# The second MLP product of five batches as seven block products, two at a time on the halves of the array

## The chip, the cores and the metric

The kernel runs on one core of one Trainium2 chip. The metric is device time in microseconds of one execution, and the median over runs is compared. Profiles come from the hardware profiler and describe one execution each.

## The reference

The computation has two stages. The first is a retention layer over 8 batches, 8 heads, 576 positions and 64 dimensions per head. Scores are multiplied by a causal decay that depends on the head, and there is no softmax. The second is a mixture-of-depths layer: in each batch a gate scores all 576 rows of 512 values, the 128 rows with the highest scores go through an MLP of 512 to 1024 to 512, and the result is added to those rows.

```
ret  = scale * (q @ k.T) * Dmat          # Dmat[i, j] = gamma_h ** (i - j) for i >= j, else 0
x    = (ret @ v), heads side by side      # (8, 576, 512)
for b in range(8):
    scores = x[b] @ w_gate
    top    = indices of the 128 largest scores
    h      = relu(x[b, top] @ w1)         # (128, 1024)
    ye     = h @ w2                       # (128, 512): the product that is changed here
    out[b] = x[b];  out[b, top] += sigmoid(scores[top])[:, None] * ye
```

Everything is fp32.

## The kernel before

**The retention stage.** The sequences are cut into chunks of 64 positions, 9 per batch, 72 in all, and two neighbouring chunks make a pair. The loop over `s` goes through 36 pairs. `block(s)` issues the matmuls of pair `s` on TensorE (PE): scores of pair `s` (L185), state updates (L175), and the products of pair `s-1` with its masked scores (L196) and with the carried state (L206). These are 64x64 tiles, and four quadrants of the array are used in turn. `masked(s)` (L242, on VectorE, called DVE) applies the causal mask to the scores, and `block(s+1)` needs its result `am`. `values(s-1)` (L251, L260) brings the outputs out of PSUM and sums them with the gate weights. ScalarE (ACT) copies states (L215); GpSimd (POOL) scales values (L161) and issues the stores. SyncE (SP) issues the loads.

**Which rows.** When a batch's scores are complete, `total` and `spread` (L293, L308) lay them out as a row. `compare` (L321, five DVE instructions per batch) counts for each score how many are larger. `one_hot` (L334, DVE) turns the ranks into the tile `hot`, and `rows` (L342, PE) multiplies it with the positions to get the indices. `gather` (L353, POOL) fetches the 128 rows from the output in HBM, into `xr`.

**The MLP.** `turn` (L370) transposes the rows on PE. `up` (L379) makes two blocks of 128 hidden units: 8 products of a 128x128 block with 128 tokens, and a relu on ACT (L381) that writes into `hT` (128 hidden units in the partitions, 8 blocks, 128 tokens). `down` (L387) multiplies two of those blocks, 128 tokens in the columns of the array, with 512 columns of `w2_sb`, into one PSUM bank `ye_ps` that collects all eight. After the eighth, one DVE instruction (L392) multiplies by the gate and adds `xr` into `o`, and POOL scatters `o` to the output (L393).

**The order.** It is written out by hand; each engine takes its instructions in the program's order. The MLP of a batch is a list of eight parts (four `up`, four `down`) in the queue `parts`. After each block, `some(n)` takes one or two of them, so MLP parts stand between blocks. The tables `before`, `mid`, `early` and `late` say what is issued at which `s`: within one `s` the order is `before`, block and mask, `mid`, values and store, `early`, the parts, `late`. `ends[b]` is 5, 9, 14, 18, 23, 27, 32 and 36. For batch `b` from 1 to 6, `total` is in `late` at `ends[b]`, `spread` and the compares at `ends[b]+1`, `one_hot` in `mid` and `rows` in `late` at `ends[b]+2`, and `turn` and the first parts at `ends[b]+4`. So the later parts of batch `b` are issued while the rows of batch `b+1` are chosen. The last parts of batch 6 and all of batch 7 come after the loop, in the tail.

PSUM tiles of the MLP and of the row choice share three banks (`bank`, tag "mm").

## Time and profile before

| | |
|---|---|
| median of the runs | 260.5 us (3 runs, 259.83 to 262.48) |
| the profiled execution | 259.97 us, its span 258.2 us |
| PE busy | 225.0 us, of which `up` (L379) 64.4 and `down` (L387) 61.4 |
| DVE busy | 133.5 us |
| ACT, POOL busy | 68.7 us, 97.6 us |
| `ye_ps` matmul of 128x512 (L387) | 128 instructions, 592 ns each from start to end |
| `o` on DVE (L392) | 8 instructions, 750 ns each |

An fp32 product is two instructions on PE, each with its weight load (PEld). Matmuls overlap, so the time from one start to the next, which the chain of waits shows, is what a product costs PE; the duration of one is longer. "Idle before" is the time an engine stood before an instruction, with the one that ended the wait. A line of the timeline reads: start, duration (both in us), engine, source line, operation, output, inputs, shapes, and in brackets the idle time before it.

### The profile page before, as it was taken

To read this page: it belongs to the slowest core of one execution; us is meant where nothing else is said; L and a number is where in the kernel's file an instruction comes from. 1 tells how busy PE (TensorE), PEld (TensorE's weight loads), DVE (VectorE), ACT (ScalarE), POOL (GpSimd) and SP (SyncE) were. 2 spreads that over 40 slices of the span, in tenths; PEclk is the share of its full clock that TensorE was granted. 3 is DMA by queue.
4 is the path that set the end of the run, shared out by engine and by line. 5 is a ranking of instruction groups with operands and counts; after the bars stand their busy time and mean duration, and the time that the engine had idled before them with its cause. 6 is when DMAs were issued, how large, how long until landed. Compare 5 with 4: busy or idle time off the path is not lost.

```text
span 258.2 us, 11519 instructions
## 1 busy us (share of the span) xinstructions
PE 225.0 (87%) x5143; PEld 178.1 (69%) x5143; DVE 133.5 (52%) x354; ACT 68.7 (27%) x230; POOL 97.6 (38%) x132
## 2 busy tenths in 40 slices
PE   0757774896996999889999998999999999999991
PEld 0746654896656797569867976689769966874940
DVE  0344696052993439546835376559465494650201
ACT  2111373131240233313511334133412342221200
POOL 4336304333363541635083722551455505301101
PEclk9995998599797999999999999999999999999997
DMA  6887999999999898799789888986133214201101
GB/s 204 278 256 260 300 371 274 384 326 327 323 287 349 287 313 289 247 310 320 232 282 307 295 280 257 322 287 196 48 83 84 60 27 127 81 3 41 41 0 41
DMA packets 28240, 56.81 MB, mean 220 GB/s; under 512 B 4128, under 2 KB 4256, under 8 KB 28192
## 3 DMA queue, kind: packets, MB, share of 16 engines
q1 hardware_dynamic: 23328, 42.46, 50.3%
q0 software_dynamic: 4864, 13.64, 15.7%
q8 instruction: 40, 0.66, 1.0%
q14 instruction: 8, 0.07, 0.1%
HBM read 44.54 MB, written 11.53 MB: 217 GB/s over the span
## 4 chain that ended last, share of the span: by engine, by line
PE 69%; issue 11%; DMA 9%; ACT 3%; DVE 3%; POOLq 1%; POOL 1%; SPq 0%; ACTq 0%
PE h_ps L379 21%; PE ye_ps L387 16%; PE u_ps L175 10%; PE sc_ps L185 8%; DMA raw<-in_qkvk 7%; PE y_ps L206 5%; PE y_ps L196 3%; PE row_ps L308 3%; DMA xr<-out,idx 2%; PE xg_ps L370 2%; DVE scr L321 2%; ACT vs L157 1%; PE rs_ps L293 1%; PE idx_ps L342 1%; POOLq L564 1%
## 5 line engine op out<-in xcount | busy, mean ns | idle before, releaser
L242 DVE TENSOR_TENSOR am<-sc_ps,table 128x512 f32<-128x512 f32 x36 | 24.9, 691 | 81.4 <-PE sc_ps L185 67.4
L379 PEld LDWEIGHTS h_ps<-xg,w_sb 128*128 128x128 f32 x512 | 61.5, 197 | 5.7 <-issue 3.3
L379 PE MATMUL h_ps<-xg,w_sb 128*128 128x128 f32 x512 | 64.4, 284 | 0.9 <-ACT xg L371 0.7
L387 PE MATMUL ye_ps<-w_sb,hT 128*128 128x512 f32 x128 | 61.4, 611 | 0.0
L185 PE MATMUL sc_ps<-raw 64*64 64x64 f32 x1152 | 45.0, 227 | 10.1 <-DMA raw<-in_qkvk 7.2
L268 POOL DMA_DIRECT2D out<-xs x64 | 39.5, 620 | 35.6 <-DVE xs L251 35.5
L175 PE MATMUL u_ps<-vs,raw 64*64 64x64 f32 x1024 | 45.2, 228 | 6.6 <-ACT st L215 3.1
L185 PEld LDWEIGHTS sc_ps<-raw 64*64 64x64 f32 x1152 | 40.1, 141 | 13.5 <-issue 12.4
L196 PE MATMUL y_ps<-vs,am 64*64 64x64 f32 x1152 | 44.7, 225 | 5.1 <-issue 4.1
L175 PEld LDWEIGHTS u_ps<-vs,raw 64*64 64x64 f32 x1024 | 37.1, 140 | 14.7 <-issue 7.6
L215 ACT COPY st<-u_ps 128x256 f32<-128x256 f32 x64 | 23.8, 372 | 88.0 <-PE u_ps L175 59.7
L196 PEld LDWEIGHTS y_ps<-vs,am 64*64 64x64 f32 x1152 | 38.4, 137 | 5.9 <-issue 4.9
L161 POOL TENSOR_TENSOR vs<-raw,table 128x512 f32<-128x512 f32 x27 | 29.1, 1079 | 34.2 <-DMA raw<-in_qkvk 27.7
L206 PE MATMUL y_ps<-st,raw 64*64 64x64 f32 x1024 | 40.5, 227 | 1.3 <-issue 1.3
L321 DVE SCALAR_TENSOR_TENSOR scr<-row,rs,ahead 128x576 f32<-128x576 f32 (+5 forms) x47 | 34.8, 741 | 8.5 <-ACT row L313 5.8
L206 PEld LDWEIGHTS y_ps<-st,raw 64*64 64x64 f32 x1024 | 36.3, 142 | 0.8 <-issue 0.7
L387 PEld LDWEIGHTS ye_ps<-w_sb,hT 128*128 128x128 f32 x128 | 22.8, 195 | 19.5 <-issue 18.5
L260 DVE SCALAR_TENSOR_TENSOR scr<-xs,table 128x256 f32<-128x256 f32 x72 | 33.7, 468 | 2.5
L353 POOL DMA_INDIRECT xr<-out,idx x8 | 8.4, 1053 | 56.4 <-ACT idx L345 56.4
L381 ACT ACTIVATE hT<-h_ps 128x256 f32<-128x256 f32 x32 | 12.3, 383 | 52.8 <-PE h_ps L379 52.8
L251 DVE TENSOR_TENSOR xs<-y_ps,table 128x512 f32<-128x512 f32 (+1 forms) x37 | 24.7, 668 | 2.8 <-PE y_ps L206 2.5
L393 POOL DMA_INDIRECT out<-o,idx x8 | 9.5, 1189 | 25.6 <-DVE o L392 24.5
(34 smaller groups left out, 110.1 us busy)
## 6 DMA issues: line engine op xcount, KB each, us to landing
raw<-in_qkvk SPq DMA_DIRECT2D x144, 256.0 KB, 4.6
out<-xs POOLq DMA_DIRECT2D x64, 128.0 KB, 4.8
w_sb<-in_w SPq DMA_DIRECT2D x16, 256.0 KB, 5.6
out<-xs POOLq DMA_DIRECT2D x16, 64.0 KB, 4.4
wg<-in_w_gate SPq DMA_DIRECT2D x1, 256.0 KB
table<-in_consts SPq DMA_DIRECT2D x1, 234.5 KB
xr<-out,idx POOLq DMA_INDIRECT x8, 5.8
out<-o,idx POOLq DMA_INDIRECT x8, 4.0
```

Of the source, the lines that this page charges most:

```text
L161: nc.gpsimd.tensor_tensor(out=blocks(vs[s]), in0=blocks(raw[s][:, 2, :]), in1=dec[:, 0, HH * c : HH * c + H].unsqueeze(2).to_broadcast([P, ...
L175: yield lambda h=h, half=half: nc.tensor.matmul(u_ps[b][half, where(0, h)], raw[s][half, 3, where(e, h)], vs[s][half, where(e, h)], start= ...
L185: yield lambda e=e, h=h, half=half: nc.tensor.matmul(sc_ps[s][half, where(e, h)], raw[s][half, 1, where(e, h)], raw[s][half, 0, where(e, h ...
L196: yield lambda e=e, h=h, i=i, half=half: nc.tensor.matmul(y_ps[s][halves[1 - i], where(e, h)], am[s][half, where(e, h)], vs[s][half, where ...
L206: yield lambda g=g, e=e, h=h, i=i, half=half: nc.tensor.matmul(y_ps[s][halves[1 - i], where(e, h)], raw[s][half, 0, where(e, h)], st[g - 1 ...
L242: nc.vector.tensor_tensor(out=blocks(am[s]), in0=blocks(sc_ps[s]), in1=causal.unsqueeze(1).to_broadcast([P, H, C]), op=OP.mult)
L251: nc.vector.tensor_tensor(out=blocks(xs[s])[:, i0:i1, :], in0=blocks(y_ps[s])[:, i0:i1, :], in1=dec[:, 1, HH * c + i0 : HH * c + i1].unsqu ...
L260: nc.vector.scalar_tensor_tensor(scr, xs[s][:, W * e : W * e + W], 1.0, wgh, op0=OP.mult, op1=OP.mult, accum_out=sc[b][:, c : c + 1])
L268: nc.gpsimd.dma_start(out=outs[b][C * c : C * c + 2 * C, W * i : W * i + W] .rearrange("(c p) d -> p c d", c=2), in_=xs[s][half, :].rearra ...
L321: nc.vector.scalar_tensor_tensor(scr[:n, : j1 - j0], row[b][:n, j0:j1], rs[b][:n, k : k + 1], ahead[:n, at + j0 : at + j1], op0=OP.subtrac ...
L379: nc.tensor.matmul(t[:, a, :], w1_sb[:, d, P * (f + a) : P * (f + a) + P], xg[b][:, d, :], start=d == 0, stop=d == KD - 1)
L387: nc.tensor.matmul(ye[b], hT[b][:, a, :], w2_sb[:, a, :], start=a == 0, stop=a == FB - 1)
```

## The change

For batches 3 to 7, `down` is replaced by `seven`, which computes the same product from blocks. Tokens are cut into two halves of 64, hidden units into two halves of 512 (four blocks of 128), output columns into two halves of 256. The usual way has eight products of such blocks; here there are seven, of sums and differences of blocks (Strassen's scheme in a variant with few sums), and sums of their results.

- `weights(i)`, i from 0 to 3, computes the four combinations of `w2` once (128x1024 each, on DVE), at the end of `late` at s=15, 16, 17 and 18.
- `hidden_sums(b)` computes four combinations of hidden blocks (128x256 each, on DVE), issued ahead of the first step of each batch.
- `product` is four matmuls (one for each block of 128 hidden units) of 64 tokens with 256 columns, into the lower or the upper 64 partitions of PSUM. `both` interleaves two such products, one on each half of the array's columns. Steps 0, 1 and 2 are two products each. Step 3 is the seventh product, cut in two halves of two blocks each, one on each half of the array.
- `add` multiplies one result (64x256) by the gate and adds it into `o`; there are eleven for a batch (2, 3, 4 and 2 after the four steps) instead of one instruction of 128x512.
- Two PSUM banks hold the results of a batch, instead of one. Some results collect in a bank where an earlier product was left.

The number of parts stays eight per batch, and the parts take the same places.

```diff
@@ -118,6 +118,7 @@
     w1_sb = const.tile([P, KD, F], F32, name="w1_sb")
     w2_sb = const.tile([P, FB, DM], F32, name="w2_sb")
     place = const.tile([P, NK], F16, name="place")
+    w2_sums = const.tile([P, 4, FB // 2, DM // 2], F32, name="w2_sums")
 
     dec = table[:, : col["causal"]].rearrange("p (s h) -> p s h", s=2)
     causal = table[:, col["causal"] : col["causal"] + C]
@@ -394,11 +395,96 @@
             out=outs[b], out_offset=bass.IndirectOffsetOnAxis(ap=idx[b][:, :1], axis=0),
             in_=o, in_offset=None)
 
+    w2_part = lambda i, j: w2_sb[:, FB // 2 * i : FB // 2 * i + FB // 2,
+                                 DM // 2 * j : DM // 2 * j + DM // 2]
+    w2_sum = lambda i: w2_sums[:, i]
+    def weights(i):
+        a, b = ((w2_part(0, 1), w2_part(0, 0)), (w2_part(1, 1), w2_sum(0)),
+                (w2_part(1, 1), w2_part(0, 1)), (w2_part(1, 0), w2_sum(1)))[i]
+        nc.vector.tensor_tensor(out=w2_sum(i), in0=a, in1=b, op=OP.subtract)
+    h_sums, o, prods = {}, {}, {}
+    h_part = lambda b, t, i: hT[b][:, FB // 2 * i : FB // 2 * i + FB // 2, C * t : C * t + C]
+    h_sum = lambda b, i: h_sums[b][:, i]
+    def hidden_sums(b):
+        h_sums[b] = work.tile([P, 4, FB // 2, C], F32, name="h_sums", bufs=1)
+        for i, (x, y, op) in enumerate((
+                (h_part(b, 1, 0), h_part(b, 1, 1), OP.add),
+                (h_sum(b, 0), h_part(b, 0, 0), OP.subtract),
+                (h_part(b, 0, 0), h_part(b, 1, 0), OP.subtract),
+                (h_part(b, 0, 1), h_sum(b, 1), OP.subtract))):
+            nc.vector.tensor_tensor(out=h_sum(b, i), in0=x, in1=y, op=op)
+    def product(b, x, w, t, to, rows=range(FB // 2), start=False):
+        for i, a in enumerate(rows):
+            yield lambda i=i, a=a: nc.tensor.matmul(
+                to[halves[t], :], x[:, a, :], w[:, a, :], start=start and i == 0, stop=True,
+                skip_group_check=True)
+    def both(x, y):
+        for f, g in zip(x, y):
+            f()
+            g()
+    def add(b, t, j, of, half, first=False):
+        at = o[b][halves[t], DM // 2 * j : DM // 2 * j + DM // 2]
+        x = xr[b][halves[t], DM // 2 * j : DM // 2 * j + DM // 2] if first else at
+        nc.vector.scalar_tensor_tensor(at, of[halves[half], :], gate[b][halves[t]], x,
+                                       op0=OP.mult, op1=OP.add)
+    def seven(b, step):
+        n = DM // 2
+        if step == 0:
+            ye[b] = [bank("ye_ps"), bank("ye_ps")]
+            o[b] = work.tile([P, DM], F32, name="o", bufs=2)
+            hidden_sums(b)
+        p, q = ye[b]
+        if step == 0:
+            both(product(b, h_part(b, 0, 0), w2_part(0, 0), 1, p[:, :n], start=True),
+                 product(b, h_part(b, 0, 1), w2_part(1, 0), 0, p[:, :n], start=True))
+            add(b, 0, 0, p[:, :n], 1, True)
+            add(b, 0, 0, p[:, :n], 0)
+        elif step == 1:
+            both(product(b, h_sum(b, 2), w2_sum(2), 1, q[:, :n], start=True),
+                 product(b, h_sum(b, 0), w2_sum(0), 0, q[:, :n], start=True))
+            add(b, 1, 1, q[:, :n], 1, True)
+            add(b, 1, 1, q[:, :n], 0)
+            add(b, 0, 1, q[:, :n], 0, True)
+        elif step == 2:
+            both(product(b, h_sum(b, 1), w2_sum(1), 1, p[:, :n]),
+                 product(b, h_sum(b, 3), w2_part(1, 1), 0, p[:, n:]))
+            add(b, 0, 1, p[:, n:], 0)
+            add(b, 0, 1, p[:, :n], 1)
+            add(b, 1, 1, p[:, :n], 1)
+            add(b, 1, 0, p[:, :n], 1, True)
+        else:
+            m = FB // 4
+            both(product(b, h_part(b, 1, 1), w2_sum(3), 1, q[:, :n], range(m)),
+                 product(b, h_part(b, 1, 1), w2_sum(3), 0, q[:, n:], range(m, 2 * m)))
+            add(b, 1, 0, q[:, n:], 0)
+            add(b, 1, 0, q[:, :n], 1)
+            nc.gpsimd.indirect_dma_start(
+                out=outs[b], out_offset=bass.IndirectOffsetOnAxis(ap=idx[b][:, :1], axis=0),
+                in_=o[b], in_offset=None)
+    SEVEN = range(3, B)
     parts = deque()
 
     def mlp(b):
         parts.extend((up, b, f) for f in range(0, FB, 2))
-        parts.extend((down, b, f) for f in range(0, FB, 2))
+        if b in SEVEN:
+            parts.extend((seven, b, i) for i in range(4))
+        else:
+            parts.extend((down, b, f) for f in range(0, FB, 2))
 
     def some(n):
         for _ in range(min(n, len(parts))):
@@ -497,6 +583,8 @@
         plan(early, s + 4, mlp, b)
         plan(late, s + 4, gates, b)
         start.append(s + 4)
+    for i in range(4):
+        plan(late, ends[2] + 1 + i, weights, i)
     plan(late, NS - 1, total, last, 0, NC - 2)
     plan(before, NS, spread, last, columns(0, odd) + [(odd, 0, C)])
     for k in range(odd):
```

In the built program the DVE queue around the first step reads, for batches 3 and 5: the values of the pair, four `hidden_sums`, two `add`, five compares, the next mask, `hot`. For batch 4, `hot` and the values come ahead of the sums.

## The prediction

> **What bounds the kernel now.** I read the page first (busy shares, then the chain), then the stretches of 20 us, then the order of events around the place where the new work lands.

> ```profile
> PE 225.0 (87%) x5143; PEld 178.1 (69%) x5143; DVE 133.5 (52%) x354; ACT 68.7 (27%) x230; POOL 97.6 (38%) x132
> PE 69%; issue 11%; DMA 9%; ACT 3%; DVE 3%; POOLq 1%; POOL 1%; SPq 0%; ACTq 0%
> ```

> ```profile
> 140.00:160.00 20.00, 19.99 (x505) 16.59 (x504) 12.66 (x33) 6.78 (x25) 7.57 (x11) 1.00 0.86 279
> 200.00:220.00 20.00, 19.59 (x514) 15.02 (x513) 12.68 (x34) 6.90 (x25) 6.84 (x11) 1.00 0.28 69
> ```

> The second fence holds stretches of 20 us: PE, weight loads, DVE, ACT, POOL, PE clock, DMA share. From 80 to 230 us PE is never idle for long, so PE time saved there is worth its full length. DVE is busy 63% of that time; this leaves room on average, but DVE is an in-order queue, so the question is what lies behind each new instruction. Here are the chain of waits, and then DVE's and ACT's order of events, around block s=24 and s=25 (the 24th and 25th pairs of chunks), where the second product of batch 3 begins:

> ```profile
> 151.27 1.98 PE h_ps L379 x16
> 153.25 1.72 PE ye_ps L387 x4
> 154.97 0.20 PE u_ps L175 x2
> ...
> 157.00 1.91 PE ye_ps L387 x4
> 158.91 0.19 PE idx_ps L342 x5
> ```

> ```profile
> 152.12 0.81 DVE L321 SCALAR_TENSOR_TENSOR scr<-row,rs,ahead 128x576 f32<-128x576 f32 x1
> ...
> 156.31 0.08 DVE L321 DVE_READ_ACCUMULATOR scr<-row,rs,ahead 64x1 f32 x1
> 156.56 0.69 DVE L242 TENSOR_TENSOR am<-sc_ps,table 128x512 f32<-128x512 f32 x1 [0.18 <-PE sc_ps L185]
> 157.17 0.87 DVE L334 TENSOR_TENSOR hot<-slots,rank 128x512 f16<-128x512 f32 x2
> ```

> ```profile
> 153.29 0.38 ACT L381 ACTIVATE hT<-h_ps 128x256 f32<-128x256 f32 x1 [1.48 <-PE h_ps L379]
> ```

> DVE compares (L321, five) from 152.12, masks (L242), and writes `hot` by 158.04. PE takes `hot` into `rows` (L342) at 158.91. The slack is 0.87 us. At s=33 and s=34, where batch 5's second product begins, the picture is the same: compares from 205.51, mask at 209.88, `hot` done at 211.36, `rows` at 212.22.

> The price of a long PE gap is in stretches of 2 us (PE busy comes first, the clock is third from the end):

> ```profile
> 78.00:80.00 2.00, 0.03 (x4) 0.03 (x4) 0.26 (x2) 0.00 (x0) 1.32 (x3) 1.00 1.02 394
> 80.00:82.00 2.00, 2.00 (x100) 2.00 (x102) 0.20 (x1) 0.37 (x1) 0.37 (x1) 0.78 0.97 349
> 82.00:84.00 2.00, 2.00 (x19) 1.79 (x18) 1.64 (x5) 0.18 (x1) 0.23 (x1) 0.50 0.88 291
> 84.00:86.00 2.00, 2.00 (x7) 0.85 (x6) 0.44 (x3) 0.40 (x1) 1.00 (x2) 0.87 0.70 210
> ```

> A gap of 2.2 us (77.8 to 79.97) is followed by a granted clock of 0.78, 0.50, 0.87: 2 x (0.22 + 0.50 + 0.13) = 1.7 us of PE work lost. The gap at 60.6 is followed by 0.51 and 0.64: 2 x (0.49 + 0.36) = 1.7 us again. After the gap of 1.2 us at 110.5 the clock stays at 1.00.

> [...]a block's 128 matmuls of 64x64 take 154.97 to 157.00, 15.9 ns each, where 64 columns at the 512-column pace (1.72 us / 4 = 430 ns) would take 54 ns, so 3.4 tiles run at once, some on the same rows.[...] the trace has 691 ns at N=512[...] and 414 ns for 128x256 on L251.

> **The change, part by part.**

> *PE work removed.* A `down` part is four instructions of 512 columns (each product is two instructions), 1.72 us. A `seven` step of four block pairs is 16 instructions of 256 columns, two at a time: 8 x 215 = 1.72 us, the same. The fourth step has two pairs: 0.86 us. That is 0.86 us saved per batch. For batches 3 to 6 PE is the bound where the step stands, at s=27, 31, 36 and in the tail: 4 x 0.86 = -3.4 us. Batch 7 is below.

> *Mode switches added.* Blocks are 64x64, `up`, `turn` and `rows` are 128-wide, and the new steps lie between them in a third mode. A `down` part after a block takes 1.91 instead of 1.72 us. One switch is thus 0 to 0.19 us; I take 0.15, with 0.3 as the upper end[...]. Two each at s=27, 29, 31, 36 and three in the tail are on the path: 11 x 0.15 = +1.7. Those at s=24, 25, 33 and 34 lie inside the wait that follows.

> *DVE's queue at s=24 and s=33.* `hidden_sums` (four tensor_tensor of 128x256) and two `add` are queued ahead of the five compares, the mask and `hot`. The sums wait for the last relu, which ended at 153.67. Four at 0.40 us (0.41 less the small overlap of neighbours): 155.27. The two adds (64x256 from PSUM: 0.75 us of L392[...], 0.48 us, each reading what the last wrote) take 1.0 us: 156.27; the product they read ends near 155.0. Then compares as before, 205.51 to 209.88 = 4.37 us: 160.64. Mask and `hot`, 209.88 to 211.36 = 1.48 us: 162.12. PE reaches `rows` at about 159.2 and finds `hot` missing; everything behind `rows` on PE waits. `rows` starts at 162.2 instead of 158.91: +3.3. At s=33: relu ends near 206.98, +1.6, +1.0, +4.37, +1.48 = 215.4 instead of 212.22: +3.2. Together +6.5 us. What I don't know is whether an add that depends on its neighbour costs more (0 to 0.1 each, twice).

> *The clock after these gaps.* PE idles about 2.9 us at each. Both gaps over 2 us between 46 and 230 us cost 1.7; the one of 1.2 us cost nothing. Bounds 0 to 1.7 each; I take 1.7: +3.4.

> *A credit.* Within the blocks at 160 and 165 us PE stands 0.83 and 0.48 us for reasons that the profile doesn't show. If those are late data or instructions, a delay of 3 us ahead of them removes them: 0 to -1.3, I take -0.6.

> *`weights`.* Four tensor_tensor of 1024 columns[...]. The first stands behind the compares of s=15: `hot` there ends at 103.3, with it 104.5, against `rows` at 104.15: +0.4. Those at s=16, 17 and 18 stand after the block's mask and values; DVE has 3.4 to 4.9 us of work in 5.4 us there: nothing, bounded by 0.5.

> *Batch 4, and the other adds.* Its sums come at s=29 after `hot`. Mask 0.6, `hot` 0.9, values 1.6, sums 1.6, adds 1.0 make 5.7 us against PE's block 2.0, h 1.9, step 1.7 and rows 0.2; the nine later adds spread over s=30 and 31 behind masks that are ready when the next block asks. Cost nothing; the cover is one `up` part or one block (2 us).

> *Tail.* The sums of batch 6 fit beside step 0 (1.7 us), its adds beside the gather for batch 7 (PE has a gap there at 236). For batch 7, from the last `up` matmul: relu done at +0.6, sums to +2.2, first adds to +3.2. PE's steps end at +1.95, +3.7, +5.4, +6.3. Adds of step 1 end at +5.3, the four of step 2 at +7.5, the two of step 3 at +8.5. Before: 245.81 to 253.68 = 7.87. The last work is DVE's: +0.6, and none of batch 7's 0.86 is gained.

> **Sum**, against the profiled execution (259.97 us; span 258.2): -3.4 + 1.7 + 6.5 + 3.4 - 0.6 + 0.4 + 0.6 = +8.6, so 268.6. The median of the runs is 260.5, 0.2% above that execution; I say 268.5.

> **Rivals.**
> 1. *The clock holds.* Same waits, gaps too short or wrongly placed for the throttle: 268.6 - 3.4 = 265, and with the full credit and cheap switches 262 to 263. For: 1.2 us cost nothing. Against: two out of two longer ones did.
> 2. *Halves of the array don't run at once.* Then a step is 3.44 us, and batch 4 alone loses 5.2 us; batches 3 and 5 hide most of two steps in the wait, 6 partly under the gather: 275 to 285. For: no row of the trace has 128x64 tiles with long moving data. Against: 15.9 ns per small matmul.
> 3. *PE's saving decides, faster.* Were `hot` late by less than its slack, -3.4 + 1.7 - 0.6 + 0.6 + 0.4 would leave 258.7, with free switches 257. It takes sums and adds that delay the compares by less than 0.9 us; the wait for the relu (153.67 against 152.12) alone takes 1.5. The point from which it decides is a delay of about 2 us, where loss and gain cancel.

> **Chances.** Forecast 0.56, first rival 0.25, second 0.10, third 0.09. Within 1% (2.6 us, about what a measurement of this kernel can tell from no change) fall the lower edge of the first rival and part of the third: same 0.09, faster 0.06, slower 0.85. Range: low, clock free and half of the credit and switches, 263; high, switches at 0.3, no credit and slower adds, 268.6 + 1.7 + 0.6 + 0.5 and some of the second rival, 273.

> **What would show it.** In the new profile: PE idle before `rows` (L342), released by `hot`, near 3 us, twice; a clock near 0.5 after each; a step in 1.7 to 1.9 us, the last in 0.9; DVE's adds as the last work. It is wrong if `rows` doesn't wait, if steps take over 3 us, or if PE waits for sums elsewhere.

## The result and the profile after

The changed kernel takes 269.2 us (median of 6 runs, 266.62 to 273.68) where the kernel before took 260.5 in the same comparison (6 runs, 257.63 to 266.17): 8.8 us more, which is 1.034 times the time before. The ratios that are given here and below compare the fast runs of each kernel alone, so they differ from the quotients of the medians; here the ratio is 1.046, with a 95% interval from 1.040 to 1.052. The forecast, 268.5, was one of the median. The profiled execution of the changed kernel took 273.68 us and lies at the long end of its runs, so single stages are compared below, and not its whole span.

First the page of the changed kernel: busy time with its share of the span, then the chain of waits by engine.

```profile
PE 224.1 (82%) x5343; PEld 183.5 (67%) x5343; DVE 168.6 (62%) x428; ACT 68.8 (25%) x230; POOL 98.5 (36%) x132
PE 59%; issue 14%; DVE 10%; DMA 10%; ACT 2%; POOLq 1%; POOL 1%; SPq 0%; ACTq 0%
```

PE's busy time hardly moved (225.0 to 224.1 us). DVE's grew by 35.1 us, and its share of the chain grew from 3% to 10%. The waits of PE between 44 and 250 us of the changed kernel show where it entered (the line that waited, the line that released it; us in total, times, longest):

```profile
PE idx_ps L343 <- DVE hot L335: 5.4, 2, 2.7
...
PE rs_ps L294 <- DVE scr L261: 1.1, 1, 1.1
```

PE stands twice before `rows` until DVE has written `hot`, and once before `total` until DVE has summed the gate scores. The kernel before had neither wait. The chain of waits through the first of the two (start, length, what), at batch 3's first `seven` step:

```profile
156.19 2.00 PE h_ps L380 x16
158.21 0.39 ACT hT L382
158.63 0.43 DVE h_sums L423
159.09 0.49 DVE h_sums L423 x2
...
159.77 0.42 DVE h_sums L423
160.22 0.49 DVE o L441
160.74 0.48 DVE o L441
161.21 0.74 DVE scr L322 x2
...
164.57 0.82 DVE scr L322 x2
...
165.92 0.68 DVE hot L335
...
166.65 0.38 PE idx_ps L343 x5
```

The chain leaves PE at the last hidden units, goes through the relu on ACT to the four sums and two adds on DVE, then through the five compares and `hot`, and only then back to PE. The timelines give both ends of the detour: DVE stands idle for the relu, with the compares queued behind the sums, and PE stands before `rows` (the idle time is in brackets). DVE of the changed kernel:

```profile
158.63 0.42 DVE L423 TENSOR_TENSOR h_sums<-hT 128x256 f32<-128x256 f32 x1 [1.50 <-ACT hT L382]
```

PE of the changed kernel, batches 3 and 5, and then the wait of `total`:

```profile
166.65 0.38 PE L343 MATMUL idx_ps<-place,hot 128*128 128x1 f16 x5 [2.69 <-DVE hot L335]
...
224.89 0.38 PE L343 MATMUL idx_ps<-place,hot 128*128 128x1 f16 x5 [2.69 <-DVE hot L335]
...
230.28 0.28 PE L294 MATMUL rs_ps<-sc,table 128*64 128x4 f32 x4 [1.06 <-DVE scr L261]
```

To compare kernels without the noise of their beginnings, I cut each trace at the start of `rows` for batches 3, 4, 5, 6 and 7. The stretches from one to the next, in us:

| kernel | 3 to 4 | 4 to 5 | 5 to 6 | 6 to 7 | 7 to end | 5 to end |
|---|---|---|---|---|---|---|
| before | 29.34 | 24.74 | 28.57 | 20.07 | 26.07 | 74.71 |
| after | 33.06 | 26.53 | 31.71 | 20.75 | 26.36 | 78.82 |
| e35: batches 3 and 5 alone | 32.08 | 23.89 | 31.54 | 20.50 | 26.09 | 78.13 |
| e467: batches 4, 6, 7 | 33.34 | 23.87 | 28.72 | 20.32 | 26.53 | 75.57 |
| e467b: the same again | 28.90 | 26.27 | 28.73 | 20.32 | 26.55 | 75.60 |
| e_dve: DVE's load alone | 33.32 | 24.53 | 31.47 | 21.40 | 26.04 | 78.91 |
| e_pe: PE's part alone | 30.94 | 23.10 | 28.26 | 19.76 | 24.61 | 72.63 |
| e_pool: sums on POOL | 30.89 | 27.51 | 30.86 | 21.79 | 26.36 | 79.01 |
| e_fill: moved behind two compares | 32.25 | 27.83 | 30.06 | 20.76 | 26.31 | 77.13 |
| e_fill2: adds moved behind `hot` too | 30.79 | 25.36 | 29.05 | 23.27 | 25.53 | 77.85 |
| e_fill346: the same without 5 and 7 | 31.03 | 26.32 | 28.73 | 20.33 | 25.59 | 74.65 |

Spans are given to 0.1 us, so the last two columns are good to 0.05 us.

Up to 180 or 190 us, while chunks are still loaded, every trace, the one of before too, has gaps of PE of up to 2.7 us that no release explains, and their number and place change from run to run. The traces show what most of them are. The pages of before and after count the packets that bring instructions (packets, MB, share):

```profile
q8 instruction: 40, 0.66, 1.0%
q8 instruction: 42, 0.69, 1.1%
```

PE of the kernel before has 5143 matmuls and as many weight loads, and 0.66 MB are 64 bytes for each of them; so a packet of 16 KB holds 256. I counted them in the 12 traces. Ahead of the matmul that ends a gap stand, in 77 gaps of 0.35 us or more, 193 or 194 more than a multiple of 256, and each of these gaps ends 0.9 to 1.6 us after such a packet has landed. So I read these gaps as PE's waits for its own next instructions. From 44 us on these gaps sum to 7.7 us in before and 10.7 in after, but also to 10.6 in e467 and 8.2 in e467b, which are the same kernel. So columns 3 to 4 and 4 to 5 carry a noise of a few us, and no run tells whether the change makes these gaps longer. The stretch from `rows` of batch 5 to the end has none of them and is the one that I lean on.

### The profile page after: what moved, and what is told of

Same layout as the page of the kernel before. It is cut to its first block, busy times and chain, and to the rows that moved or that the text cites. A ratio compares the mean times of both kernels' runs of the same rounds, so it can differ in the third digit from the quotient of the medians.

```text
span 272.0 us, 12010 instructions
## 1 busy us (share of the span) xinstructions
PE 224.1 (82%) x5343; PEld 183.5 (67%) x5343; DVE 168.6 (62%) x428; ACT 68.8 (25%) x230; POOL 98.5 (36%) x132
## 4 chain that ended last, share of the span: by engine, by line
PE 59%; issue 14%; DVE 10%; DMA 10%; ACT 2%; POOLq 1%; POOL 1%; SPq 0%; ACTq 0%
PE h_ps L380 20%; PE u_ps L176 8%; PE sc_ps L186 7%; DMA raw<-in_qkvk 7%; PE ye_ps L388 7%; DVE scr L322 5%; PE ye_ps L428 5%; PE y_ps L207 4%; PE y_ps L197 3%; DMA xr<-out,idx 3%; PE xg_ps L371 2%; PE row_ps L309 2%; DVE scr L261 1%; DVE xs L252 1%; DVE o L441 1%
## 5 line engine op out<-in xcount | busy, mean ns | idle before, releaser
L380 PE MATMUL h_ps<-xg,w_sb 128*128 128x128 f32 x512 | 65.9, 286 | 4.3 <-issue 3.3
L176 PE MATMUL u_ps<-vs,raw 64*64 64x64 f32 x1024 | 46.3, 229 | 8.7 <-issue 3.9
L176 PEld LDWEIGHTS u_ps<-vs,raw 64*64 64x64 f32 x1024 | 37.7, 140 | 14.4 <-issue 7.2
L261 DVE SCALAR_TENSOR_TENSOR scr<-xs,table 128x256 f32<-128x256 f32 x72 | 33.2, 461 | 2.5
L354 POOL DMA_INDIRECT xr<-out,idx x8 | 9.0, 1127 | 63.3 <-ACT idx L346 63.3
L388 PE MATMUL ye_ps<-w_sb,hT 128*128 128x512 f32 x48 | 23.6, 619 | 0.0
L428 PE MATMUL ye_ps<-w_sums,h_sums 128*64 128x256 f32 x120 | 18.8, 384 | 0.0
L158 ACT ACTIVATE vs<-raw,table 128x64 f32<-128x64 f32 x72 | 18.2, 337 | 0.0
```

Source lines behind the costliest of these rows:

```text
L176: yield lambda h=h, half=half: nc.tensor.matmul(u_ps[b][half, where(0, h)], raw[s][half, 3, where(e, h)], vs[s][half, where(e, h)], start= ...
L261: nc.vector.scalar_tensor_tensor(scr, xs[s][:, W * e : W * e + W], 1.0, wgh, op0=OP.mult, op1=OP.mult, accum_out=sc[b][:, c : c + 1])
L380: nc.tensor.matmul(t[:, a, :], w1_sb[:, d, P * (f + a) : P * (f + a) + P], xg[b][:, d, :], start=d == 0, stop=d == KD - 1)
L388: nc.tensor.matmul(ye[b], hT[b][:, a, :], w2_sb[:, a, :], start=a == 0, stop=a == FB - 1)
L428: yield lambda i=i, a=a: nc.tensor.matmul(to[halves[t], :], x[:, a, :], w[:, a, :], start=start and i == 0, stop=True, skip_group_check=True)
```

## The experiments

Theory A is that of the prediction: the sums of batches 3 and 5, which wait for the last relu, and the first adds stand in DVE's queue ahead of the compares and `hot`, and PE waits for `hot`. The rivals put the time on PE itself (half-array steps and changes of tiling mode), or in the clock and the gaps while chunks are loaded.

**Batches 3 and 5 alone, and the other three alone.**

```diff
-    SEVEN = range(3, B)
+    SEVEN = (3, 5)        # e35
+    SEVEN = (4, 6, 7)     # e467, e467b
```

> Only batches 3 and 5 by seven products. Theory A (PE waits in rows for hot, because sums and adds stand ahead of the compares; only batches 3 and 5 have that order): before plus 5 to 7 us, so 265.5 to 267.5, with two gaps near 2.7 us ahead of rows. Rival B (each batch pays evenly on PE, by more instructions and switches of the tiling mode): two fifths of the 8.8 us, before plus 3.5.

> Only batches 4, 6 and 7 by seven products. Theory A: before minus 1 to plus 2 us, no wait for hot over 1 us. Rival B: three fifths of the 8.8 us, before plus 5.3.

> Batches 4, 6 and 7 by seven products once more, in more rounds, since its first time disagreed with its own stages. Theory A: before minus 1 to plus 2 us. Rival B: before plus 5.3.

e35 took 265.25 us (4 runs, 261.97 to 271.43) against 259.43 of before beside it (7 runs, 253.54 to 264.55): +5.8. PE's waits between 44 and 250 us of e35:

```profile
PE idx_ps L343 <- DVE hot L335: 5.4, 2, 2.7
...
PE rs_ps L294 <- DVE scr L261: 1.1, 1, 1.1
```

Two batches bring all three waits back at the same size. e467 took 263.53 (4 runs, 258.25 to 263.74) against the same 259.43, and yet has none of these waits (before `total` PE stands once for 0.5 us, at 62 us, ahead of everything that was changed). So the medians of four runs don't separate the two kernels, and the traces have to. The table places its excess between `rows` of 3 and 4 (33.34 us), ahead of any instruction that differs in batch 4, in a gap of 2.40 us, one of those for instructions, and half a clock after it (the mean clock is 0.959 in this trace and 0.977 in that of e467b, below). Since no edit lies there, the same kernel was run once more, beside other runs of before: 260.53 (6 runs) against 261.36 (11 runs), ratio 1.012 [0.997, 1.028], and 28.90 us in that stretch. Batches 4, 6 and 7 together cost no more than about 1 us in the trace (75.60 against 74.71 from `rows` of 5 on), half of it in the tail. Theory A holds: most of the cost sits in batches 3 and 5.

**Each engine's part by itself.** e_pe keeps PE's instructions of all five batches, but leaves out `weights`, `hidden_sums` and all adds: products take plain blocks, and two DVE instructions per batch write `o`, so sums of blocks are missing from the result.

```diff
-    w2_sum = lambda i: w2_sums[:, i]
+    w2_sum = lambda i: w2_part(i // 2, i % 2)
-    h_sum = lambda b, i: h_sums[b][:, i]
+    h_sum = lambda b, i: h_part(b, i // 2, i % 2)
...
-            hidden_sums(b)
-            add(b, 0, 0, p[:, :n], 1, True)
...
+            for j, t in enumerate((p, q)):
+                nc.vector.scalar_tensor_tensor(
+                    o[b][:, n * j : n * j + n], t[:, :n], gate[b], xr[b][:, n * j : n * j + n],
+                    op0=OP.mult, op1=OP.add)
...
-    for i in range(4):
-        plan(late, ends[2] + 1 + i, weights, i)
```

> The PE instructions of the changed kernel, but blocks of hidden units and of w2 in place of all sums, and two DVE instructions of 128x256 per batch in place of eleven adds (sums of blocks and most adds are left out). Theory A: 257 to 260.5, PE's own cost is a small gain. Rival B: 266 or more, the loss is in the PE instructions.

e_dve is the kernel before, with DVE work of the same size (four of 128x256 that read `hT`, two of 64x256) behind the first `down` part of batches 3 and 5.

```diff
+        for i, (x, y) in enumerate(((part(1, 0), part(1, 1)), (spare[:, 0], part(0, 0)),
+                                    (part(0, 0), part(1, 0)), (part(0, 1), spare[:, 1]))):
+            nc.vector.tensor_tensor(out=spare[:, i], in0=x, in1=y, op=OP.subtract)
+        spare2 = work.tile([P, 256], F32, name="spare2", bufs=1)
+        for x in (xr[b][:C, :256], spare2[:C, :]):
+            nc.vector.scalar_tensor_tensor(spare2[:C, :], xr[b][:C, 256:], gate[b][:C], x,
+                                           op0=OP.mult, op1=OP.add)
...
+        if f == 0 and b in (3, 5):
+            loaded(b)
```

> The kernel before, with DVE work of the same size added behind the first down part of batches 3 and 5 alone: four sums of 128x256 of hidden blocks, two instructions of 64x256 on rows, results unused. Theory A: before plus 5.5 to 6.5 us, with two gaps near 3 us ahead of rows. Rival B: within 1 us of before.

e_pe took 260.13 us (4 runs, 257.16 to 262.79) against 259.43, a difference that four runs can't tell from none. Its trace has no wait for `hot`, and from `rows` of batch 5 on it is 2.1 us shorter than before. e_dve took 266.22 (4 runs, 263.33 to 271.79) against 259.43: +6.8. First the timeline of DVE in e_dve, then that of PE:

```profile
150.67 0.42 DVE L388 TENSOR_TENSOR spare<-hT 128x256 f32<-128x256 f32 x1 [1.50 <-ACT hT L381]
```

```profile
158.56 0.38 PE L342 MATMUL idx_ps<-place,hot 128*128 128x1 f16 x5 [2.69 <-DVE hot L334]
```

With PE's program untouched, six DVE instructions behind one part give the same wait for the relu (1.50 us) and the same gap of PE (2.69 us) as the change. The rivals on PE fall: in the trace, PE's part alone gains a little. e_pe also prices it. From `rows` of 5 to that of 7 it gains 0.6 us on before, about 0.3 for each of two batches, and 1.5 us from there to the end, where the last steps of batch 6 and all of batch 7 lie and DVE has only two instructions left to do. The tail of the changed kernel gains nothing of it.

**The work moved out of the way.** If position in the queue is the cause, the same work behind part of the compares must cost less. In e_fill the sums of batches 3 and 5 and their first two adds are issued behind the second compare. e_fill2 puts the adds behind `hot` and leaves batch 7 to `down`. e_fill346 is e_fill2 with batch 5 left to `down` as well.

```diff
+        if k == 2:
+            for f, *x in pending:
+                f(*x)
+            pending.clear()
...
-            hidden_sums(b)
+            if b in (3, 5):
+                pending.append((hidden_sums, b))
+            else:
+                hidden_sums(b)
...
-    SEVEN = range(3, B)
+    SEVEN = range(3, B - 1)   # e_fill2
+    SEVEN = (3, 4, 6)         # e_fill346
```

> The changed kernel with the sums and the first two adds of batches 3 and 5 moved behind the second compare, so that two compares fill the wait for the relu. Theory A: the gap ahead of rows falls from 2.69 to about 1.2 us (less by the 1.5 us that DVE waited for the relu), twice; time 265 to 268. Were the gap set by PE or a load, it would stay at 2.69.

> The changed kernel with the sums of batches 3 and 5 behind the second compare, their first two adds behind hot, and batch 7 by the old product. Theory A: the gap ahead of rows falls below 0.3 us (2.69 less 1.5 for the filled wait less 1.0 for the two adds), and from rows of batch 5 to the end it is 73.5 to 75 us, against 74.7 in the kernel before and 78.8 in the changed one; time from 2 us below to 1 us above the kernel before. Were the gap set by something else, it stays near 1 us.

> The kernel with filled wait and late adds, but batch 5 by the old product too, so seven products for batches 3, 4 and 6 alone. Theory A with DVE's backlog as the second step (the adds of batch 5 delay the gate sums that rs_ps of the last batch waits for): the wait ahead of rs_ps (1.90 us) falls below 0.3, from rows of batch 5 to the end 73.5 to 75.5 us instead of 77.9, time within 2.5 us of the kernel before. If something else in the new steps costs the rest, 4 us or more above it remain.

e_fill took 266.26 us (before: 261.36; ratio 1.026 [1.004, 1.048]). The wait for the relu is filled by two compares, and the two gaps shrink from 5.4 to 2.0 us together. PE's waits in e_fill:

```profile
PE idx_ps L347 <- DVE hot L339: 2.0, 2, 1.1
```

In e_fill2 the wait for `hot` is gone, and yet the kernel took 267.3 us against 260.28 (ratio 1.028 [1.013, 1.044]), where its expectation had about the time of before. The timeline of PE in e_fill2, and then two of its stretches (length; PE, weight loads, DVE, ACT, POOL; PE clock, DMA share, GB/s):

```profile
222.42 0.28 PE L294 MATMUL rs_ps<-sc,table 128*64 128x4 f32 x4 [1.90 <-DVE scr L261]
```

```profile
219.80:223.22 3.42, 1.10 (x13) 0.48 (x10) 3.32 (x9) 0.31 (x2) 1.18 (x2) 1.00 0.28 83
223.22:226.63 3.41, 3.41 (x50) 2.96 (x52) 2.63 (x8) 0.53 (x1) 0.00 (x0) 0.50 0.28 60
```

The gap of PE has moved from `rows` of batch 6 to `total` of batch 7, one pair of chunks later. DVE's queue in e_fill2 shows why:

```profile
216.17 0.48 DVE L450 SCALAR_TENSOR_TENSOR o<-ye_ps,gate,xr 64x256 f32<-64x256 f32 x1
216.69 0.48 DVE L450 SCALAR_TENSOR_TENSOR o<-ye_ps,gate,o 64x256 f32<-64x256 f32 x1
...
218.73 0.49 DVE L450 SCALAR_TENSOR_TENSOR o<-ye_ps,gate,xr 64x256 f32<-64x256 f32 x1
219.26 0.48 DVE L450 SCALAR_TENSOR_TENSOR o<-ye_ps,gate,o 64x256 f32<-64x256 f32 x1
219.75 0.48 DVE L450 SCALAR_TENSOR_TENSOR o<-ye_ps,gate,xr 64x256 f32<-64x256 f32 x1
220.16 0.67 DVE L243 TENSOR_TENSOR am<-sc_ps,table 128x512 f32<-128x512 f32 x1
...
221.93 0.43 DVE L261 SCALAR_TENSOR_TENSOR scr<-xs,table 128x256 f32<-128x256 f32 x1
```

Five adds stand between `hot` and the last pair's gate sums (L261), which `total` needs. After this gap the clock is 0.50 for 3.41 us, so half of that, 1.7 us of PE work, goes as well. Gap and clock, 3.6 us, cover what this trace takes more than before from `rows` of batch 5 on (3.1 us). The other 3.5 us by which its span is longer lie earlier, in the noisy part, and this wait doesn't explain them. With batch 5 left out (e_fill346) both waits are gone: 260.88 us against 260.77, ratio 1.010 [1.002, 1.019], and 74.65 us from `rows` of 5 on, against 74.71 before. So the changed kernel's waits can be undone one by one, but what is then left of the saving isn't visible.

**The sums on POOL.** In e_pool the sums of batches 3 to 5 run on GpSimd, and adds are issued with the next step. e_pool6 is the same with batch 7 left to `down`.

```diff
-            nc.vector.tensor_tensor(out=h_sum(b, i), in0=x, in1=y, op=op)
+            (nc.gpsimd if b < 6 else nc.vector).tensor_tensor(out=h_sum(b, i), in0=x, in1=y, op=op)
...
+    def add(*a):
+        waiting.append(a)
...
+    def flush():
+        while waiting:
+            add_now(*waiting.popleft())
...
-    SEVEN = range(3, B)
+    SEVEN = range(3, B - 1)   # e_pool6
```

> The changed kernel with the sums of batches 3 to 5 on POOL and every step's adds issued on DVE at the next step, so that nothing new stands ahead of the compares. Theory A: no wait for hot over 0.5 us, the stretch from rows of batch 4 to the end some 6 us shorter than in the changed kernel, time 259 to 263. Rival B (cost on PE in each batch): no shorter than 267.

> As the one with sums on POOL, and batch 7 by the old product. Theory A: 258 to 262, the tail from rows of batch 7 to the end 0.3 to 0.9 us shorter than in the changed kernel. Rival B: 265 or more.

Here my expectation missed. e_pool took 266.43 us (ratio 1.034 [1.023, 1.045]), and e_pool6 264.34 (1.027 [1.014, 1.041]), both against 261.36. The waits of PE between 44 and 250 us of e_pool:

```profile
PE ye_ps L428 <- DVE o L450: 1.8, 3, 1.2
...
PE idx_ps L343 <- DVE hot L335: 0.9, 3, 0.6
PE h_ps L380 <- DVE o L450: 0.8, 1, 0.8
...
PE rs_ps L294 <- DVE o L450: 0.6, 1, 0.6
```

The wait for `hot` fell from 5.4 to 0.9 us as expected, but the adds, now later, hold the PSUM banks that PE wants next, 3.2 us in all. The compares lost part of what they had gained, too. First DVE in e_pool, then POOL:

```profile
216.47 1.18 DVE L322 SCALAR_TENSOR_TENSOR scr<-row,rs,ahead 128x576 f32<-128x576 f32 x1
...
217.69 1.16 DVE L322 SCALAR_TENSOR_TENSOR scr<-row,rs,ahead 128x576 f32<-128x576 f32 x1
```

```profile
216.30 0.73 POOL L423 TENSOR_TENSOR h_sums<-hT 128x256 f32<-128x256 f32 x1 [0.86 <-ACT hT L382]
...
219.40 1.74 POOL L423 TENSOR_TENSOR h_sums<-hT,h_sums 128x256 f32<-128x256 f32 x1
```

Beside POOL's sums a compare takes 1.16 to 1.18 us, where the first at 214.75 us took 0.81, and POOL's sums grow from 0.73 to 1.74 us. e_pool6 takes 0.74 us less than e_pool from `rows` of batch 7 to the end (25.62 against 26.36), the price of `seven` in the tail, which the prediction had at 0.6.

## Why the prediction was right, and where it wasn't

*DVE's queue at s=24 and s=33 (+6.5): right, and a little too high.* PE was to idle about 2.9 us at each and idled 2.69. The stretches grew by 3.7 and 3.1 us, where +3.3 and +3.2 stood; only the second shows anything, since the first lies in the noisy part (e467 has 33.34 us there without this wait). e_dve makes the same gap without any other part of the change, e_fill shrinks it by moving the same instructions, and e467b hasn't got it. The relu's part came out exactly as read from the kernel before: 1.50 us of DVE idle, where the two times in the profile of before differ by 1.55. The 0.48 us that the forecast had for an add is what the kernel before lets one estimate: 0.75 us for 512 columns (L392) less 0.27, by which L251 takes longer for 512 columns (682 ns) than for 256 (414). In the changed kernel the 55 adds took 471 to 492 ns.

*PE work removed and switches added (-3.4 and +1.7): right in mechanism, somewhat less of a gain.* The chain of the changed kernel at batch 4 (start, length, what):

```profile
189.39 1.98 PE h_ps L380 x16
191.37 1.88 PE ye_ps L428 x16
...
195.74 3.60 PE ye_ps L428 x32
...
201.96 1.01 PE ye_ps L428 x8
202.97 1.98 PE h_ps L380 x16
```

A step takes 1.88 us and not 1.72, the last one 1.01 and not 0.86, and the `up` part after it 1.98, where 1.78 followed a `down` part before. Two steps in a row take 3.60 = 1.88 + 1.72, so the 0.16 comes once for a change of mode and not with each step. So the halves of the array do work at once (the second rival falls; that step would take 3.44 us), and a change of mode costs 0.15 to 0.20, close to the 0.15 that was taken; the upper end of 0.3 was my estimate, and no run shows a change at that price. The net gain that e_pe shows is about 0.3 us per batch; the sum had 0.43 (1.7 over four batches).

*The clock after these gaps (+3.4): mis-sized.* Here the reasoning failed: half a clock was taken as sure after each gap of this length. In the profiled execution of the changed kernel the clock didn't drop after either gap. In e35 it dropped after the first. These are stretches of 3.41 us of the changed kernel around both gaps, and of e35 around its first (PE busy comes second, the clock third from the end):

```profile
162.17:165.59 3.42, 1.79 (x16) 0.90 (x14) 3.31 (x9) 2.28 (x9) 0.00 (x0) 1.00 0.61 217
165.59:169.00 3.41, 2.35 (x133) 2.29 (x133) 3.27 (x10) 0.53 (x2) 1.50 (x2) 1.00 0.41 130
...
220.20:223.61 3.41, 2.00 (x25) 1.06 (x16) 3.28 (x9) 2.29 (x9) 0.00 (x0) 1.00 0.00 0
223.61:227.02 3.41, 2.13 (x126) 2.09 (x130) 3.31 (x11) 0.53 (x2) 1.28 (x2) 1.00 0.02 5
```

```profile
156.63:160.04 3.41, 1.16 (x12) 0.48 (x8) 3.30 (x10) 1.66 (x7) 0.00 (x0) 1.00 0.78 252
160.04:163.45 3.41, 2.97 (x105) 2.95 (x109) 3.26 (x10) 0.53 (x2) 2.11 (x3) 0.50 0.78 252
```

Of the six gaps of 2.69 us in the traces of after, e35 and e_dve, two were followed by half the clock, at 1.7 us each (3.41 us at half). In these traces the two kinds differ in where the gap lies. In each of the 12 traces the stretches at half the clock begin at whole multiples of 3.41 us from each other (in before at 64.05 and 81.11 us, 5 x 3.41 apart; in after at 114.38 and 179.24 us, 19 x 3.41 apart), as if the time were cut into slices of 3.41 us. By my count, between 50 and 245 us, all 12 slices in which PE stood for 1.84 us or more were followed by half the clock (2.19 and 2.17 us in before, 1.95 and 1.96 in after), none with less than 1.5 us was, and 3 of 23 in between. In the changed kernel the edge of a slice cut both gaps, into 1.6 and 1.1 us and into 1.4 and 1.3; in e35 2.25 us of the first fell into one slice. A gap of 2.69 us that begins anywhere in a slice has 1.84 us of it in one slice in 2.4 of 3.41 cases. So my estimate from these figures is 0.7 x 1.7 for each gap, +2.4 for both on average, not +3.4. Two out of two in the kernel before was too little to call it the rule, and two of six in these traces is fewer than that estimate. In the profiled execution it was the first rival that came true; it gave 265 there, and the time was longer for other reasons.

*"The other adds cost nothing": wrong for batches 4 and 5.* The working looked at batch 4 only. For batch 5: after `hot` of batch 6 DVE has no slack: it is busy for 1.88 us or more of every 2 between 222 and 228 us of the changed kernel, and the three adds of batch 5's step 1 push the gate sums that `total` of batch 7 waits for. That is the 1.06 us before `rs_ps`. e35 keeps it, e467b hasn't got it, and e_fill2 stretches it to 1.90 us. Batch 4 costs a smaller wait of the same kind. Its last two adds delay DVE's scores for `gates` (L362), ACT stands before the sigmoid `gate`, and behind that stands the copy of the states, after which PE's next state updates start:

```profile
206.41 0.20 ACT L363 ACTIVATE gate<-g 128x1 f32<-128x1 f32 x1 [1.03 <-DVE scr L362]
```

```profile
206.97 0.68 PE L176 MATMUL u_ps<-vs,raw 64*64 64x64 f32 x16 [0.42 <-issue]
```

The profile names no releaser for these 0.42 us. But every trace with batch 4's adds on DVE has them at this place (0.37 to 0.42 us, 0.9 in the two with late adds), and before, e35, e_pe and e_dve haven't. That the state copy is what PE waits for is my reading of this order of events; no run tests it alone.

*`weights` (+0.4): not seen.* `rows` at s=16 started without a wait for DVE. The forecast let the first end 1.2 us behind `hot` (103.3 to 104.5); L251's two sizes, extended to 1024 columns, give 1.22 us. In the changed kernel the four took 1.21, 1.22, 2.65 and 1.22 us.

*Tail (+0.6): right.* From the last `up` matmul to DVE's last add it takes 8.55 us (forecast 8.5, before 7.87). The last `up` matmuls of the changed kernel on PE, and its last work on DVE:

```profile
253.77 5.19 PE L380 MATMUL h_ps<-xg,w_sb 128*128 128x128 f32 x45
```

```profile
266.50 1.01 DVE L441 SCALAR_TENSOR_TENSOR o<-ye_ps,gate,o 64x256 f32<-64x256 f32 x2
```

*The sum.* With measured terms, and the estimate for the clock, it is 5.4 (gaps) + 1.1 (`total`) + 0.4 (state copy) + 0.7 (tail) - 1.2 (PE, 4 x 0.3) + 2.4 (clock) = 8.8 us, against the 8.8 between the medians. That it fits to the tenth is chance: the runs of each kernel scatter by 7 to 9 us, and the ratio of 1.046 would put the loss nearer to 12 us. In the trace of the changed kernel, whose clock held after both gaps, the terms from `rows` of batch 5 on (2.7 + 1.1 + 0.4 + 0.7 - 0.9) give 4.0 us, and the table has 4.1. The forecast of +8.6 came this close because errors cancelled, which is luck: the gaps, the clock and `weights` were too high by 2.5 us in all, and the gain of PE and the credit were too good by 1.1, while the waits of `total` and of the state copy (1.5 us) weren't in it. The credit of -0.6 was for two gaps that were to vanish behind the delay. They are waits for instructions, and after and e35 don't have them, but after has another of 1.96 us at 176 us.

The third rival, that PE's saving decides, needed a delay of `hot` below about 2 us. e_fill brought the wait of PE to 1 us each, and from `rows` of batch 5 on it was still 2.4 us longer than before: DVE's backlog behind it decides as well, which that rival left out. The prediction's 63% for DVE between 80 and 230 us is that of its stretch from 140 to 160 us; over the whole of that time DVE is busy for 90.2 of 150 us, 60%, and nothing rests on the difference.

## What to carry to other kernels

Before giving work to an engine that has room on average, follow its queue at that place: what the new instruction itself waits for counts with its duration, and everything behind it inherits both (1.5 us of the 4.1 here was a wait for another engine's relu). When such a wait is moved away, look for the next consumer that the backlog reaches, as `total` was here. Seven block products for eight save an eighth of the time of the MLP's second product, 0.86 of 6.9 us a batch here; eleven adds and four sums in fp32 took 11 x 0.48 + 4 x 0.42 = 7.0 us of DVE a batch, where one instruction had taken 0.75, and need a place where nobody waits.
